# An attention and MLP kernel: one slot's score groups, two mask operands, one turn, one placing and the output buffers rearranged

## The chip, the cores and the metric

The kernel runs on one core of a Trainium2 chip. The metric is the device time of one execution in microseconds; lower is better. The engines of the core are TensorE (PE in the profile, its weight loads PEld), VectorE (DVE), ScalarE (ACT), GpSimd (POOL) and SyncE (SP). Each runs its own instructions in the order in which the program gives them, and waits on semaphores for the others. GpSimd and SyncE also issue the DMAs here.

## The reference

Attention with a forgetting decay over 8 batches, 8 heads, 576 positions and a head size of 64, and behind it an MLP whose activation is h - tanh(h):

```python
scores = scale * np.matmul(q, k.transpose(0, 1, 3, 2))
log_f = np.log(np.clip(f, 0.0001, 1.0))
cum = np.cumsum(log_f, axis=-1)
decay = cum[:, :, :, None] - cum[:, :, None, :]
scores = np.where(causal, -1000000000.0, scores + decay)
scores = scores - np.max(scores, axis=-1, keepdims=True)
attn = np.exp(scores)
attn = attn / (np.sum(attn, axis=-1, keepdims=True) + 1e-09)
x = (attn @ v), heads side by side, as 4608 rows of 512
h = x @ w_in                      # 512 x 2048
out = (h - np.tanh(h)) @ w_out    # 2048 x 512
```

## The kernel before

**Slots.** The 64 heads are worked on in 32 pairs, four to a batch. The program is a sequence of slots, one for each pair p (0 to 31) and one more to finish. In slot p the scores of pair p are made, their exponentials taken, and the values of pair p - 1 multiplied; MLP steps fill the rest. The order of all five engines is the order in which the program emits instructions (a manual schedule).

**Scores.** A pair's scores are laid into seven tiles (`TILES`, 0 to 6) of up to 512 columns, transposed: keys on the partitions, queries along the columns. Each tile has a PSUM bank, an exponential on ScalarE (L358) and, from slot 5 on, a causal mask by GpSimd on the result (L369). In slots 0 to 4 the mask is a further matmul instead (L350), of two 128 x 128 operands: `neg16`, which is -32768 on the diagonal and 0 elsewhere, and `tri16`, which is 32768 where the column is smaller than the row and 0 elsewhere. Both lie in space that weight sums use later, and are filled once at the start (L163 and L164, then L171 and L173 on GpSimd). The decay rides along as three further rows of the operands KT and QT, which come from the running sum `cum` (L178). In the slots of batch 0 tiles go in groups, `GROUPS`: g0 is tiles 0 and 1, g1 is 2 and 4, g2 is 5 and 6, g3 is tile 3. A group of two takes a double bank of a pool of two; g3 takes one of two turning banks (`t_bank`), which transposes also use.

**The hand-written order.** `FIRST` lists what slots 0 to 4 emit: `g0` to `g3` and `s0` to `s6` are score groups and tiles, `va` and `vb` the values of the two heads of the pair before, `q1` and `k1` the transposes of the next pair's q and k, `y` and `x` the turn of a finished pair's result into XR, `r` and `c` rows of constants, `m` an MLP step. From slot 5 on, `att_items` emits the seven score tiles of the slot, behind each tile the loads that `LOADS` holds for it, behind tile 1 the values and the turn of the pair before, and behind two tiles given by `TURNED` (0 and 3 where it has no entry) the transposes of q and of k for the next pair. Between these items MLP steps are spread evenly, `TAKEN` of them or 7 to 8.

**Values.** `values` makes 15 matmuls for each head (L379) into one PSUM tile; behind the second head VectorE takes the reciprocal of the sum (L385, L386) and writes `xn` (L387).

**Loads and turns.** q, k, v and the weights come in converting DMAs on GpSimd's queue. For batches 0 to 2 q and k are turned by TensorE (`trans`, L289) and copied to QT and KT by VectorE or ScalarE (L299, L297). From batch 3 on (`FAR`) they come in blocks, five for q and five for k, SyncE's queue turns them by DMA (L100) into TQ and TK, and VectorE copies them to the rows of QT and KT, four copies for each (`place`, L103: argument a is the head of a pair, c the first of two pairs). For a batch b these copies are due in the last slot of the batch before; for batch 3 that is slot 11: q behind tiles 0 and 1, k behind tiles 4 and 5, for c = 0 and c = 2 alike.

**MLP.** Finished rows are taken in nine units of 512. For each of a unit's 16 feature tiles `mlp1` makes four matmuls (L414) into a bank of a pool of three, ScalarE makes the tanh (L421), and VectorE adds it (L427) to make `gt`. The second matrix product is made of seven products of half-size blocks (`product`, L462), with sums of gt (`sums`, L441) and of the weights (`wsum`, L271). `settle` takes a product out of PSUM: three of them go to a part in SBUF, four complete a quarter of the unit's output in a tile `ost` and store it from SyncE's queue (L493). `ost` comes from the pool `tmp`, which has two buffers for each tag:

```python
ost = tmp.tile([P, DM], FP32, tag="th" if half == 0 and n == 4 else "ost", name="ost") if half != 1 else PART.pop((u, n, "ost"))
```

In the last unit two quarters are stored in halves (L486, L487), and the fourth takes a tanh buffer.

Of the kernel before, what the change touches and what calls it, by code (L numbers as in the profile page):

```python
# [8 lines left out]
FP32 = mybir.dt.float32  # L9
FP16 = mybir.dt.float16  # L10
AF = mybir.ActivationFunctionType
ALU = mybir.AluOpType
PE = mybir.EngineType.PE

PITCH = 640
VW = 66
SHIFT = 5.0
FAR = 3
BIG = 32768.0
# [4 lines left out]
def kernel(  # L24
# [10 lines left out]
    nc = tc.nc  # L35
    P = 128

    B, H, S, D = q.shape
    NH = B * H
    DM, DFF = moe_w_in.shape  # L40
    NT = B * S
    assert D == 64 and DM == H * D and S == 4 * P + 64 and H % 2 == 0
    NPAIR = H // 2
# [15 lines left out]
    smp = ctx.enter_context(tc.tile_pool(name="smp", bufs=NFT // 4))  # L59
    prt = ctx.enter_context(tc.tile_pool(name="prt", bufs=3))  # L60
    tmp = ctx.enter_context(tc.tile_pool(name="tmp", bufs=2))
    PSUM = bass.MemoryType.PSUM
    ps_av = ctx.enter_context(tc.tile_pool(name="ps_av", bufs=1, space=PSUM))
    ps_tr = ctx.enter_context(tc.tile_pool(name="ps_tr", bufs=1, space=PSUM))
# [37 lines left out]
    def place(dst, src, b, a, c):  # L102
        nc.vector.tensor_copy(out=dst[b % 2][0:D, 2 * c + a:2 * c + 3 + a:2, 0:S], in_=src[a * D:(a + 1) * D, c:c + 2, :])  # L103
# [39 lines left out]
    def load_aug(b, h0=0):  # L143
# [16 lines left out]
    nc.vector.memset(pick[0:1, 1:2], 1.0)  # L160
    nc.vector.memset(cqs[NH:P, :], 0.0)
    nc.vector.memset(KT[0][D:D + 3, 0, :], 0.0)
    nc.vector.memset(neg16, 0.0)  # L163
    nc.vector.memset(tri16, 0.0)  # L164
    nc.vector.tensor_scalar(out=lf, in0=lf, scalar1=0.0001, scalar2=1.0,
                            op0=ALU.max, op1=ALU.min)
    nc.vector.memset(QT[0][D:D + 3, 0, :], 0.0)
    nc.vector.memset(KT[0][0:D, :, S:PITCH], 0.0)
    load_qk(qn, q, 0, 4, 6)
    load_qk(kn, k, 0, 4, 6)  # L170
    nc.gpsimd.affine_select(out=neg16, in_=neg16, compare_op=ALU.not_equal,  # L171
                            fill=-BIG, base=0, pattern=[[-1, P]], channel_multiplier=1)
    nc.gpsimd.affine_select(out=tri16, in_=tri16, compare_op=ALU.is_ge,  # L173
                            fill=BIG, base=0, pattern=[[1, P]], channel_multiplier=-1)
    nc.scalar.activation(out=lf, in_=lf, func=AF.Ln)
    first = cst.tile([1, 1], FP32)
    nc.scalar.activation(out=first, in_=lf[0:1, 0:1], func=AF.Exp)
# [54 lines left out]
    def at_tile(p, ti, load):  # L232
        LOADS.setdefault((p + ti // 7, ti % 7), []).append(load)
# [10 lines left out]
    for b in range(2, B):  # L244
        p0 = (b - 1) * NPAIR
        late = 7 * (b == FAR)
        for n in range(NJ):
            at_tile(p0, (13, 15, 18, 22, 24)[n] if b == 2 else 7 + n + late, lambda b=b, n=n: load_v_part(b, n))
        if b > 2:
            at_tile(p0, 0, lambda b=b: load_aug(b))  # L250
        if b < FAR:
            continue
        for n in range(NJ):
            at_tile(p0, n - 7 + late, lambda b=b, n=n: load_block(qb, q, b, n))
            at_tile(p0, n + late, lambda b=b, n=n: load_block(kb, k, b, n))
            at_tile(p0, 4 + n + late, lambda b=b, n=n: turn_block(TQ, qb, b, n))
            at_tile(p0, 11 + n + late // 2, lambda b=b, n=n: turn_block(TK, kb, b, n))
        for n, (dst, src) in enumerate(((QT, TQ), (KT, TK))):
            for a in range(2):
                for c in (0, 2):  # L260
                    at_tile(p0 + 3, 2 * n + a + late // 3 * n, lambda b=b, dst=dst, src=src, a=a, c=c: place(dst, src, b, a, c))

    E, XN, AV, HP, GT, GP, M2, SUM, PART = {}, {}, {}, {}, {}, {}, {}, {}, {}

# [209 lines left out]
    def settle(u, n, ps, half=None):  # L474
        r0, e0 = u * UW + T2 * (n in (4, 7)), E2 * (n in (3, 7))
        if n in (1, 6, 5):
            part = prt.tile([P, DM], FP32, tag="part", name="part")
            PART[(u, n)] = part
            nc.scalar.activation(out=part, in_=ps, func=AF.Copy)  # L479
            return  # L480
        ost = tmp.tile([P, DM], FP32, tag="th" if half == 0 and n == 4 else "ost", name="ost") if half != 1 else PART.pop((u, n, "ost"))
        if half is not None:
            if half == 0:
                PART[(u, n, "ost")] = ost
            cols = slice(half * E2, half * E2 + E2)
            nc.vector.tensor_tensor(out=ost[:, cols], in0=ps[:, cols], in1=PART[(u, {7: 5, 4: 6}[n])][:, cols], op=ALU.add)  # L486
            nc.sync.dma_start(out=out[r0 + half * P:r0 + half * P + P, e0:e0 + E2], in_=ost[:, cols])  # L487
            return
        if n == 3:
            nc.scalar.activation(out=ost, in_=ps, func=AF.Copy)  # L490
        else:
            nc.vector.tensor_tensor(out=ost, in0=ps, in1=PART.pop((u, {2: 1, 7: 5, 4: 6}[n])), op=ALU.add)  # L492
        nc.sync.dma_start(out=out[r0:r0 + T2, e0:e0 + E2].rearrange("(g p) e -> p g e", p=P),  # L493
                          in_=ost.rearrange("p (g e) -> p g e", g=2))
# [15 lines left out]
    def step():  # L510
        for fn, *args in mlp[STEPS[0]]:
# [1 line left out]
        STEPS[0] += 1  # L513

    FIRST = [["8", "q0", "2", "k0", "3", "p", "s0", "s1", "q1", "s2", "k1", "s4", "s5", "q2", "s6", "s3"],
# [36 lines left out]
            else:  # L552
                spin(int(what))

    TURNED = {2 * NPAIR - 1: (3, 5), 2 * NPAIR + 1: (1, 4)}
    TAKEN = {NPAIR + 1: 5, NPAIR + 2: 5, 2 * NPAIR - 1: 5, 2 * NPAIR: 8, 2 * NPAIR + 1: 8}

    def att_items(p):
# [65 lines left out]
```

## Time and profile before

| | us |
|---|---|
| median of 3 runs | 346.81 (346.33 to 347.29) |
| the profiled execution | 345.82 |
| its span, first to last instruction | 344.1 |
| granted TensorE clock, mean | 1.000 |

The profile is of one execution. Its page gives the busy time of each engine and its share of the span; a timeline row gives an instruction's start and length, its engine and line, what it writes and reads, and in brackets how long the engine had been idle and what ended that. Busy times overlap between engines, so that an engine's idle time matters only where the others wait for it.

### The profile page before, as it was taken

How to read it: one execution, taken by the hardware profiler on the slowest of the kernel's cores; microseconds unless marked ns; L12 is line 12 of the kernel's file. 1: busy time of each engine (PE TensorE's matmuls, PEld its weight loads, DVE VectorE, ACT ScalarE, POOL GpSimd, SP SyncE). 2: the span in 40 equal slices, each digit the busy share in tenths (PEclk: the TensorE clock that was granted, in tenths of full speed). 3: DMA queues.
4: the chain of work that ended last, by engine and by line, in shares of the span. 5: the costliest groups of instructions: out<-in, count | busy, mean ns of one | idle time of the engine just before them, and what ended most of it. 6: DMA issues, size and time to landing. Idle time of an engine off the chain costs nothing.

```text
span 344.1 us, 8654 instructions
## 1 busy us (share of the span) xinstructions
PE 331.9 (96%) x3297; PEld 232.4 (68%) x3297; DVE 252.5 (73%) x521; ACT 219.4 (64%) x412; POOL 178.8 (52%) x325
## 2 busy tenths in 40 slices
PE   7899999989999999999999999999999999999996
PEld 2675557855578557887886568656887786486475
DVE  7576989749893789477965898488848864873872
ACT  6676878748655886578657875687558843633631
POOL 8987577954777637772767367742322220500500
PEclk9999999999999999999999999999999999999999
DMA  9999999999999969999999999992131013002003
GB/s 97 146 183 173 195 192 146 129 173 132 146 104 158 178 116 92 132 178 128 89 111 169 164 78 118 175 159 52 54 102 18 19 48 104 0 25 100 3 0 124
DMA packets 169560, 38.82 MB, mean 113 GB/s; under 512 B 155906, under 2 KB 169454, under 8 KB 169518
## 3 DMA queue, kind: packets, MB, share of 16 engines
q0 software_dynamic: 116576, 18.36, 86.2%
q1 hardware_dynamic: 52942, 19.90, 29.4%
q8 instruction: 26, 0.43, 0.5%
q14 instruction: 16, 0.13, 0.2%
HBM read 36.85 MB, written 9.44 MB: 135 GB/s over the span
## 4 chain that ended last, share of the span: by engine, by line
PE 80%; DVE 6%; DMA 4%; POOL 3%; ACT 2%; SPq 2%; issue 1%; POOLq 0%; DVEq 0%
PE mb L414 30%; PE px L462 16%; PE mb L462 15%; PE ps L342 11%; PE av L379 8%; DVE gt L427 2%; SPq L100 2%; DMA vn<-in_v_dram 2%; DMA TQ<-qn 1%; DMA kn<-in_k_dram 1%; ACT e L358 1%; DVE sm L441 1%; POOL vn L114 1%; ACT th L421 1%; PE t L289 1%
## 5 line engine op out<-in xcount | busy, mean ns | idle before, releaser
L414 PE MATMUL mb<-XR,win 128*128 128x512 f16 (+4 forms) x704 | 141.4, 340 | 2.1 <-DVE ost L492 1.1
L358 ACT ACTIVATE e<-ps 128x512 f16<-128x512 f32 (+1 forms) x183 | 109.0, 619 | 21.2 <-PE ps L342 13.3
L421 ACT ACTIVATE th<-mb 128x512 f32<-128x512 f32 x144 | 86.5, 601 | 53.0 <-PE mb L414 45.4
L427 DVE TENSOR_TENSOR gt<-mb,th 128x512 f16<-128x512 f32 x144 | 97.2, 687 | 23.4 <-ACT th L421 22.5
L369 POOL TENSOR_SCALAR_AFFINE_SELECT e<-e 128x128 f16<-128x128 f16 x162 | 60.2, 375 | 100.1 <-ACT e L358 99.2
L414 PEld LDWEIGHTS <-win 128*128 128x128 f16 x704 | 61.8, 97 | 50.4 <-issue 4.1
L342 PE MATMUL ps<-QT,KT 67*128 67x448 f16 (+4 forms) x376 | 73.7, 278 | 2.5 <-ACT th L421 0.8
L462 PEld LDWEIGHTS <-gt 128*128 128x128 f16 x576 | 53.8, 97 | 11.9 <-DVE gt L427 2.0
L342 PEld LDWEIGHTS <-KT 67*128 67x128 f16 x384 | 36.3, 98 | 24.6 <-DVE KT L299 2.9
L462 PEld LDWEIGHTS <-sm 128*128 128x128 f16 x432 | 40.4, 97 | 6.7 <-issue 0.4
L462 PE MATMUL mb<-ws,gt 128*128 128x256 f16 x288 | 36.4, 272 | 0.0
L379 PEld LDWEIGHTS <-e 128*128 128x128 f16 x896 | 32.1, 97 | 4.8 <-issue 1.3
L379 PE MATMUL av<-vn,e 128*128 128x65 f16 x896 | 33.8, 193 | 1.3 <-DMA vn<-in_v_dram 0.9
L492 DVE TENSOR_TENSOR ost<-mb,part 128x512 f32<-128x512 f32 x25 | 17.2, 686 | 22.7 <-PE mb L462 8.1
L479 ACT ACTIVATE part<-px 128x512 f32<-128x512 f32 x24 | 14.3, 597 | 29.7 <-PE px L462 29.7
L462 PE MATMUL px<-ws,sm 128*128 128x256 f16 x256 | 31.6, 272 | 0.0
L114 POOL DMA_DIRECT2D vn<-in_v_dram x32 | 28.5, 894 | 1.7 <-issue 1.2
L387 DVE TENSOR_TENSOR xn<-av,rs 128x640 f16<-128x640 f32 x32 | 26.4, 825 | 1.1
L441 POOL TENSOR_TENSOR sm<-gt 128x512 f16<-128x512 f16 x4 | 4.6, 1154 | 36.3 <-DVE gt L427 36.3
L95 POOL DMA_DIRECT2D qn<-in_q_dram x25 | 22.1, 883 | 1.5 <-issue 1.4
L462 PE MATMUL mb<-wout,gt 128*128 128x256 f16 x160 | 21.6, 273 | 0.7 <-DVE gt L427 0.7
L95 POOL DMA_DIRECT2D kn<-in_k_dram x25 | 21.4, 854 | 1.7 <-issue 1.6
(91 smaller groups left out, 302.4 us busy)
## 6 DMA issues: line engine op xcount, KB each, us to landing
out_dram<-ost SPq DMA_DIRECT2D x34, 256.0 KB
vn<-in_v_dram POOLq DMA_DIRECT2D x32, 128.0 KB, 6.1
qn<-in_q_dram POOLq DMA_DIRECT2D x20, 128.0 KB, 3.9
kn<-in_k_dram POOLq DMA_DIRECT2D x20, 128.0 KB, 4.5
win<-in_moe_w_in_dram POOLq DMA_DIRECT2D x4, 512.0 KB, 8.8
wout<-in_moe_w_out_dram POOLq DMA_DIRECT2D x2, 1024.0 KB, 16.4
qn<-in_q_dram POOLq DMA_DIRECT2D x10, 144.0 KB, 7.2
kn<-in_k_dram POOLq DMA_DIRECT2D x10, 144.0 KB, 6.8
```

The source lines that it names most:

```text
L95: nc.gpsimd.dma_start(out=dst[b % 2][0:pn, n, :].rearrange("p (h d) -> p h d", h=H), in_=src[b, :, n * P:n * P + pn, :].rearrange("h p d - ...
L114: nc.gpsimd.dma_start(out=vn[b % 2][:, n, h0:h1, 0:D], in_=v[b, h0:h1, n * P:(n + 1) * P, :].rearrange("h p d -> p h d"))
L342: nc.tensor.matmul(out=ps[:, col:col + n], lhsT=KT[b % 2][0:rows, h, j * P:(j + 1) * P], rhs=QT[b % 2][0:rows, h, i0:i0 + n], start=True, ...
L358: nc.scalar.activation(out=eb[:, :, lo:hi], in_=banks[:, 0:n2, lo:hi], func=AF.Exp, scale=qscale)
L369: nc.gpsimd.affine_select(out=view, in_=view, compare_op=ALU.is_ge, fill=0.0, base=0, pattern=pat, channel_multiplier=-1)
L379: nc.tensor.matmul(out=av[:, a, ib, :], lhsT=E.pop((b, c, a, j, ib)), rhs=vn[b % 2][:, j, 2 * c + a, 0:D + 1], start=(j == 0), stop=(j == ib))
L387: nc.vector.tensor_tensor(out=xn.rearrange("p i (a d) -> p a i d", a=2), in0=av[:, :, :, 0:D], in1=rs.to_broadcast([P, 2, NJ, D]), op=ALU. ...
L414: nc.tensor.matmul(out=hps[:, o:o + n], lhsT=win[:, ci, ft * P:(ft + 1) * P], rhs=XR[:, ci, t:t + n], start=(ci == 0), stop=(ci == NCH - 1))
L421: nc.scalar.activation(out=th, in_=hps, func=AF.Tanh, scale=-1.0)
L427: nc.vector.tensor_tensor(out=GT[(u, ft)], in0=hps, in1=th, op=ALU.add)
L462: nc.tensor.matmul(out=ps[:, g * E2:(g + 1) * E2], lhsT=left(k), rhs=right[:, k, :], start=(first and (g == 0 or last) and k == 0), stop=( ...
L492: nc.vector.tensor_tensor(out=ost, in0=ps, in1=PART.pop((u, {2: 1, 7: 5, 4: 6}[n])), op=ALU.add)
```

## The change

Six edits:

1. `tri16` and `neg16` are made by VectorE: `neg16` is the identity times -32768, and `tri16` a running sum along each row that starts at 32768 and adds `neg16`, so that it falls to 0 from the diagonal on. The two fills and the two GpSimd selects go. The fills of QT and KT that stood behind the clamp of f stand ahead of it.
2. In slot 1 the groups g3 and g2 come before `va` and `vb`.
3. In slot 5 the transposes of k come behind tile 2 instead of tile 3.
4. `ost` has a pool of its own, `osp`, with three buffers, and the last unit's fourth tile takes from it too.
5. For batch 3 the copies with c = 0 come behind tiles 2 and 3 (q) and 4 and 5 (k) of slot 11.
6. Those with c = 2 come behind tiles 0 and 1 (q) and 2 and 3 (k) of slot 12. The other batches stay as they were.

```diff
+    osp = ctx.enter_context(tc.tile_pool(name="osp", bufs=3))
...
     nc.vector.memset(KT[0][D:D + 3, 0, :], 0.0)
-    nc.vector.memset(neg16, 0.0)
-    nc.vector.memset(tri16, 0.0)
+    nc.vector.memset(QT[0][D:D + 3, 0, :], 0.0)
+    nc.vector.memset(KT[0][0:D, :, S:PITCH], 0.0)
     nc.vector.tensor_scalar(out=lf, in0=lf, scalar1=0.0001, scalar2=1.0,
                             op0=ALU.max, op1=ALU.min)
-    nc.vector.memset(QT[0][D:D + 3, 0, :], 0.0)
-    nc.vector.memset(KT[0][0:D, :, S:PITCH], 0.0)
+    nc.vector.tensor_scalar_mul(out=neg16, in0=id16, scalar1=-BIG)
+    nc.vector.tensor_tensor_scan(out=tri16, data0=ones16[:, 0:P], data1=neg16, initial=BIG,
+                                 op0=ALU.mult, op1=ALU.add)
     load_qk(qn, q, 0, 4, 6)
     load_qk(kn, k, 0, 4, 6)
-    nc.gpsimd.affine_select(out=neg16, in_=neg16, compare_op=ALU.not_equal,
-                            fill=-BIG, base=0, pattern=[[-1, P]], channel_multiplier=1)
-    nc.gpsimd.affine_select(out=tri16, in_=tri16, compare_op=ALU.is_ge,
-                            fill=BIG, base=0, pattern=[[1, P]], channel_multiplier=-1)
...
-                    at_tile(p0 + 3, 2 * n + a + late // 3 * n, lambda b=b, dst=dst, src=src, a=a, c=c: place(dst, src, b, a, c))
+                    o = 2 * n + a + (2 + 5 * (c > 0)) * (b == FAR)
+                    at_tile(p0 + 3, o, lambda b=b, dst=dst, src=src, a=a, c=c: place(dst, src, b, a, c))
...
-        ost = tmp.tile([P, DM], FP32, tag="th" if half == 0 and n == 4 else "ost", name="ost") if half != 1 else PART.pop((u, n, "ost"))
+        ost = osp.tile([P, DM], FP32, tag="ost", name="ost") if half != 1 else PART.pop((u, n, "ost"))
...
-             ["r", "g0", "k1", "g1", "va", "vb", "g3", "g2"],
+             ["r", "g0", "k1", "g1", "g3", "g2", "va", "vb"],
...
-    TURNED = {2 * NPAIR - 1: (3, 5), 2 * NPAIR + 1: (1, 4)}
+    TURNED = {NPAIR + 1: (0, 2), 2 * NPAIR - 1: (3, 5), 2 * NPAIR + 1: (1, 4)}
```

## The prediction, before the changed kernel ran

> **What bounds the kernel now.** I read the page first, then the busy time by stage, then TensorE's timeline for its waits, and last the engines around each wait.
>
> ```profile
> span 344.1 us, 8654 instructions
> PE 331.9 (96%) x3297; PEld 232.4 (68%) x3297; DVE 252.5 (73%) x521; ACT 219.4 (64%) x412; POOL 178.8 (52%) x325
> q0 software_dynamic: 116576, 18.36, 86.2%
> 70.00:80.00 10.00, 8.65 (x85) 5.30 (x84) 6.11 (x12) 5.23 (x12) 5.93 (x11) 1.00 1.59 169
> 80.00:90.00 10.00, 9.75 (x86) 5.26 (x85) 9.67 (x20) 7.57 (x16) 6.63 (x13) 1.00 1.91 143
> 110.00:120.00 10.00, 10.00 (x109) 6.03 (x107) 6.67 (x12) 7.46 (x15) 7.00 (x14) 1.00 2.33 165
> ```
>
> TensorE (PE) is busy 331.9 of 344.1 us, so at most 12.2 us can be won without taking work off it. A stage row gives start and end, the stage's length, then busy time of PE, PEld, DVE, ACT and POOL: from 110 us PE is full, and what is idle lies in the first 100. Its waits there:
>
> ```profile
> 8.17 0.39 PE L342 MATMUL ps<-QT,KT 67*128 67x512 f16 x1 [0.64 <-DVE KT L299]
> 14.84 0.43 PE L379 MATMUL av<-vn,e 128*128 128x65 f16 x9
> 16.17 0.31 PE L379 MATMUL av<-vn,e 128*128 128x65 f16 x5 [0.90 <-DMA vn<-in_v_dram]
> 43.55 0.39 PE L342 MATMUL ps<-QT,KT 67*128 67x512 f16 x1 [0.79 <-ACT th L421]
> 58.29 0.60 PE L462 MATMUL mb<-ws,sm 128*128 128x256 f16 x4 [0.22 <-DVE ws L271]
> 75.31 1.02 PE L414 MATMUL mb<-XR,win 128*128 128x512 f16 x4 [1.06 <-DVE ost L492]
> 77.09 1.02 PE L414 MATMUL mb<-XR,win 128*128 128x512 f16 x4 [0.29 <-DVE gt L427]
> 97.06 0.28 PE L462 MATMUL mb<-wout,gt 128*128 128x256 f16 x1 [0.36 <-DVE gt L427]
> 97.66 0.28 PE L462 MATMUL mb<-wout,gt 128*128 128x256 f16 x1 [0.32 <-DVE gt L427]
> 20.45 0.90 PE av L379 x30
> ```
>
> The number in brackets is the idle time before the row. It understates the loss: thirty value matmuls follow each other in 0.90 us on the chain of waits (0.03 each), so the nine at 14.84 fill 0.27 us, while their modelled end comes after 0.43. About 0.16 us belongs on top of each idle time.
>
> **Masks by VectorE.** Two mask selects leave GpSimd (POOL), where they stand ahead of the first v loads; two zero fills leave VectorE (DVE), which gets a multiply and a scan of 128 columns; two other fills move to an earlier pause of DVE.
>
> ```profile
> 3.64 0.45 DVE L165 TENSOR_SCALAR ws<-ws 64x576 f32<-64x576 f32 x1 [0.62 <-DMA ws<-in_f_dram]
> 4.12 0.68 ACT L175 ACTIVATE ws<-ws 64x576 f32<-64x576 f32 x1 [2.03 <-DVE ws L165]
> 4.84 1.35 DVE L178 TENSOR_TENSOR_SCAN ws<-ones,ws 64x576 f32<-64x576 f16 x1
> 7.17 0.45 POOL L171 TENSOR_SCALAR_AFFINE_SELECT ws<-ws 128x128 f16<-128x128 f16 x1
> 7.82 3.55 POOL L114 DMA_DIRECT2D vn<-in_v_dram  x4
> 11.34 5.27 DMA vn<-in_v_dram
> ```
>
> POOL issues v from 7.17 instead of 7.82, 0.65 sooner. The last v block lands at 11.34 + 5.27 = 16.6. The queue that carries it is busy for 86% of all engines' span, so an earlier issue is not an equally earlier landing: between 0 and 0.65 us, I take 0.3, near the middle. On DVE the two moved fills use the 0.62 us for which it stood for f (3.64) and what the removed fills free; only a rest beyond that would move the clamp. The new pair fits between the clamp, which ends when ACT's logarithm starts (4.12), and the running sum at 4.84, which waits for that logarithm (4.12 + 0.68 = 4.80). The scan by its length is 1.35 x 128/576 = 0.30 us, or 1.35 if nothing of it scales; the multiply lies between a tiny operation's 0.17 (17.32 below) and half of 1.19, a copy of 1152 columns (92.57 below); I take 0.2. The 0.5 fits into 0.7, so it costs nothing; at the upper ends it ends at 4.1 + 0.6 + 1.35 = 6.05 and delays the running sum by 1.2.
>
> A POOL issue beside DVE copies took longer than its siblings (0.89 each at 7.82):
>
> ```profile
> 92.34 1.17 POOL L95 DMA_DIRECT2D qn<-in_q_dram  x1
> 92.57 1.19 DVE L103 COPY QT<-TQ 64x1152 f16<-64x1152 f16 x2 [0.90 <-DMA TQ<-qn]
> ```
>
> The Trainium skill, SBUF — State Buffer, Who interferes with whom, says that a VectorE copy or tensor_scalar in a two-port mode and GpSimd share one port pair, and that the later one is blocked outright, descriptor writing included. The 0.28 us that this issue took longer agrees. By that rule the new multiply would hold up a q or k issue by up to its own 0.2 and the sum would be 4.4 instead of 4.5.
>
> **Slot 1's order.** The score groups g3 and g2 now come before both value halves.
>
> ```profile
> 14.16 1.94 ACT L358 ACTIVATE e<-ps 128x1024 f16<-128x1024 f32 x2 [0.20 <-PE ps L342]
> 17.32 0.17 DVE L385 TENSOR_SCALAR rs<-av 128x10 f32<-128x10 f32 x1 [1.98 <-PE av L379]
> 17.87 0.38 PE L342 MATMUL ps<-QT,KT 67*128 67x512 f16 x1
> 18.89 0.92 DVE L299 COPY QT<-t 64x576 f16<-64x576 f16 x2 [0.28 <-PE t L289]
> 20.23 0.46 DVE L398 COPY XR<-t 128x576 f16<-128x576 f16 x1 [0.43 <-PE t L397]
> ```
>
> Before, values run from 14.84 to about 17.1 (their end releases DVE's rs at 17.32); g3 and g2 fill the 0.75 to slot 2's start at 17.87. After, g3 starts at 14.84. g2 needs the score bank of g0, whose exponential, the first of two in 1.94, ends at about 15.2; so both groups end near 15.85, and the 0.90 of values at 16.75, with v's last block at 16.3 wanted at about that time. PE comes to slot 2 1.1 us sooner. What is late next is DVE: rs starts 16.95, 0.37 sooner, and its pauses of 0.28 and 0.43 close partly, since PE is further ahead. The k copies without which PE can't open the next slot come at the end of that DVE sequence, so from there PE gains what DVE gains. I take **0.9** for masks and order together; with v landing as before and no DVE pause closed it is 0.4, with all of PE's lead 1.1.
>
> **Slot 5's k a tile sooner.**
>
> ```profile
> 39.95 0.42 PE L289 MATMUL t<-id,kn 96*128 96x96 f16 x6
> 40.34 1.28 DVE L427 TENSOR_TENSOR gt<-mb,th 128x512 f16<-128x512 f32 x2
> 42.58 0.91 DVE L299 COPY KT<-t 64x576 f16<-64x576 f16 x2
> 45.94 0.69 DVE L427 TENSOR_TENSOR gt<-mb,th 128x512 f16<-128x512 f32 x1 [0.31 <-ACT th L421]
> 48.86 0.69 DVE L427 TENSOR_TENSOR gt<-mb,th 128x512 f16<-128x512 f32 x1 [0.44 <-ACT th L421]
> ```
>
> The copies end at 43.49, and PE starts slot 6 at 43.55: the row blames ACT, but the copy is what ended then. In the new order the six turns precede an MLP step, some 0.9 sooner than 39.95, and on DVE the copies stand before the second gt and two sums: they end near 41.0 + 0.9 = 41.9. PE's wait (0.79 + 0.16) goes. Behind the copies the second gt is now late by 0.9; nothing takes its bank before slot 6's first step. DVE then runs with only the pauses 0.31 and 0.44 up to the wsum that releases PE at 58.29, so no more than 0.75 can arrive there. I take **0.6**; the bounds are 0 and 1.0.
>
> **Three output buffers, and the placing of batch 3.**
>
> ```profile
> 67.52 8.14 SPq L493 DMA_DIRECT2D out_dram<-ost  x3
> 74.56 0.69 DVE L492 TENSOR_TENSOR ost<-mb,part 128x512 f32<-128x512 f32 x1 [3.15 <-DMA out_dram<-ost]
> 76.47 1.27 SPq L400 DMA_TRANSPOSE XR<-xn  x1
> 87.48 4.97 DMA TQ<-qn
> 91.38 3.88 SPq L100 DMA_TRANSPOSE TK<-kn  x3
> 99.20 0.91 DVE L103 COPY KT<-TK 64x1152 f16<-64x1152 f16 x2
> ```
>
> Unit 0's fourth output tile takes the second one's buffer, whose store was issued at 67.52; DVE stands 3.15 us for it, with rs, xn and the gt of the next unit behind, and SP's queue with the turns of xn and of batch 3. With three buffers it takes the first tile's, which the third tile already reused at two, so it runs near 71.4. The waits at 75.31 and 77.09 go: 1.06 + 0.29 + 2 x 0.16 = 1.67. DVE keeps 3.1 - 1.7 = 1.4 us of lead over PE, loses the 0.90 wait for TQ, and has two of its four q copies (half of 1.19, twice) moved into slot 12: the waits at 97.06 and 97.66, 0.36 + 0.32 + 0.32 = 1.0, go as well, and the 0.25 idle of the stage 80:90 with them. In sum 2.9; with the modelled ends of the waits in that stage **3.0**; between 1.7 (97 us stays) and 3.3. In the last unit the fourth tile, which took a tanh buffer for its halves, rotates through the three as well: it gets the first tile's, whose store is older than the one that the third waited for until now, so this costs nothing. The four moved copies, some 2.2 us, lie in slot 12, where PE has no wait; without that cover they would cost up to 2.2. What is late next is TK: SP's third issue starts near 94.0, lands 4.97 later at 99.0, and DVE places k at 99.20. SP's chain starts after xn's turn (76.47), which comes 2.9 sooner, so TK moves with PE but leaves no reserve.
>
> **Sum.** 0.9 + 0.6 + 3.0 = 4.5. The profiled execution took 345.82 us (344.1 of span, 1.7 around it): 341.3. It lies 1.0 below the median of the runs, 346.81; by the median the forecast is **342.3**. The bounds add to 2.1 and 5.4: 341.4 to 344.7.
>
> **Rivals.** (1) The loads set the front: v, and the q and k of the next batches, land when the busy queue lets them, PE runs into them, and the first two terms of the sum (1.5) are lost: 346.81 - 3.0 = 343.8. The 86% speaks for it; against it, among PE's waits shown behind 8 us only the one at 16.17 names a load. (2) TK lands no sooner than SP's chain lets it, DVE stands before slot 12 in place of the old waits at 97: third part 1.7, 346.81 - 3.2 = 343.6. For it speaks the 0.2 us margin, against it that SP is released as early as DVE. (3) The buffer is not what DVE waits for at 74.56, and only the front's 1.5 remains: 345.3. The row names the store, so this is weak. (4) Slower: scan and multiply cost their upper ends, the running sum comes 1.2 later, and the pause before the first score (8.17) grows from 0.64 to 1.84, longer than any shown inside the work. If the granted clock then fell to half for 10 us of matmuls, 5 us would be lost: 346.81 - 3.6 + 1.2 + 5 = 349.4. It decides at the length of that pause; pauses of 1.06 left the stage row at clock 1.00. The Trainium skill, TensorE: Matmul & The Clock Gate, What's actually happening, puts the fall at an idle window of about 3.4 us, so by it 1.84 would not suffice; no run here shows such a fall.
>
> **How the numbers follow.** A difference under 0.3% (1.04 us) is no change here. Chances: the forecast 57%, rival 1 18%, rival 2 13%, rival 3 5%, rival 4 5%, and 2% beyond. Faster: 57 + 18 + 13 and about half of rival 3's 5, less a little for unlucky runs: 89%. Same 5%, slower 6%. The range takes in the bounds and half a microsecond of spread between runs (346.33 to 347.29): 340.9 to 344.9, which leaves out rivals 3 and 4.
>
> **What would show it.** Masks: v's issue near 7.2 and no later running sum than 4.84. Slot 1: no wait of PE for vn over 0.3, slot 2 near 16.8. Slot 5: no wait of PE before slot 6, k's copies before the second gt. Buffers: no DVE wait for the output store near 71, and no PE waits from there to slot 12; if TK sets slot 12, a DVE wait for TK before the first L103 copy to KT. The forecast is wrong if PE's idle total falls by less than 2 us, or if PE's first score comes later than 8.2.

## The result, and the profile after

The changed kernel takes 343.78 us (median of 7 runs, 342.54 to 344.70) against 346.81 us for the kernel before in the same session (7 runs, 345.36 to 348.17). The ratio is 0.9912 with a 95% interval of 0.9883 to 0.9941, that is 2.0 to 4.1 us less. The profiled execution took 343.53 us, 2.29 less than that of before. The forecast was 342.3: the direction and the range held, and 1.5 us of the 4.5 that it promised did not come.

The page of the changed kernel, and its busy time by stage (start and end, length, then busy time of PE, PEld, DVE, ACT, POOL, the granted clock, DMA's busy share, and GB/s):

```profile
span 341.8 us, 8662 instructions
PE 330.5 (97%) x3297; PEld 232.2 (68%) x3297; DVE 254.5 (74%) x521; ACT 219.3 (64%) x412; POOL 178.6 (52%) x323
q0 software_dynamic: 116576, 18.36, 83.9%
...
50.00:60.00 10.00, 7.75 (x91) 5.80 (x90) 9.06 (x20) 7.28 (x15) 6.03 (x11) 1.00 2.51 150
70.00:80.00 10.00, 10.00 (x102) 6.44 (x101) 7.32 (x15) 6.94 (x14) 6.45 (x13) 1.00 2.07 181
80.00:90.00 10.00, 9.99 (x92) 5.39 (x90) 9.63 (x20) 8.05 (x18) 6.98 (x14) 1.00 1.93 147
90.00:100.00 10.00, 10.00 (x128) 7.97 (x125) 9.60 (x20) 6.42 (x13) 7.65 (x14) 1.00 1.75 135
```

From 70 to 100 us TensorE is now full, where before it stood 1.35 us in the stage from 70 and 0.25 in the stage from 80. In exchange the stage from 50 us has 2.25 us of idle time, where the kernel before has 0.43:

```profile
50.00:60.00 10.00, 9.57 (x107) 6.93 (x106) 9.76 (x21) 9.09 (x19) 7.21 (x13) 1.00 2.63 150
```

TensorE's timeline of the changed kernel names the waits; the number in brackets is the idle time ahead of the row and what ended it:

```profile
9.08 0.39 PE L341 MATMUL ps<-QT,KT 67*128 67x512 f16 x1 [1.27 <-DVE KT L298]
17.66 0.38 PE L341 MATMUL ps<-QT,KT 67*128 67x512 f16 x1
20.11 0.42 PE L288 MATMUL t<-id,kn 96*128 96x96 f16 x6 [0.46 <-DVE QT L298]
55.30 0.43 PE L288 MATMUL t<-id,qn 96*128 96x96 f16 x6 [1.66 <-DMA qn<-in_q_dram]
59.90 0.39 PE L341 MATMUL ps<-QT,KT 67*128 67x512 f16 x1 [0.42 <-ACT KT L296]
```

The first score comes 0.91 later than the 8.17 of before, slot 2 opens at 17.66 instead of 17.87, the wait for v's block is gone, the wait before slot 6 is gone, and a new one of 1.66 (1.83 with the 0.16 of the modelled end) stands at 55.30 for the load of batch 2's first q. How far each run's TensorE had come is best read where the values of a pair begin (30 matmuls for each pair). This table is worked out from the traces of before, after and eleven of the runs below (e5 is left out, whose start is another); "stage" is the time from pair 8's values to pair 11's, in which the output buffers matter:

```
                      first   values of pair                          stage
                      score   1      5      7      8      11          8 to 11
before                8.17   20.29  45.12  61.37  71.16  101.30       30.14
after                 9.08   20.37  44.26  62.35  72.14   99.04       26.90
e1_buffers            8.11   19.84  44.66  60.95  70.74   97.80       27.06
e2_place              8.11   20.54  45.36  61.62  71.41  101.02       29.61
e15_k_alone           8.14   20.57  44.57  62.32  72.11  102.33       30.22
e9_slot1              8.10   20.07  44.79  61.45  71.24  101.04       29.80
e8_masks              9.13   20.28  45.10  61.36  71.15  100.57       29.42
e4_k_later            9.19   20.47  45.19  61.45  71.25   98.14       26.89
e10_masks_early       8.30   20.29  44.18  63.69  73.48  100.38       26.90
e3_gpsimd_masks       8.09   20.19  44.09  62.83  72.62   99.52       26.90
e11_q_sooner          9.07   20.36  44.25  61.96  71.75   98.65       26.90
e12_q_sooner_gpsimd   8.10   20.02  43.92  60.18  69.97   98.09       28.12
e14_tk_sooner         8.11   19.94  44.36  62.92  72.71   99.61       26.90
```

Behind pair 11 all of them keep their distance to the end. So the change went like this: 0 at pair 1, 0.86 won at pair 5, 1.84 lost again by pair 7, and 3.24 won between pairs 8 and 11. That is 2.26 in all, and accounts for the two profiled executions (2.29). The medians differ by more, 3.03, because the profiled execution of the kernel before lies 1.0 below its median and that of the changed kernel 0.25; the table doesn't explain that part. The kernel before, e1, e2 and e15 have the same program up to slot 5, and their pair 1 begins between 19.84 and 20.57: a difference of half a microsecond there, between single profiles, says nothing.

VectorE's head of the changed kernel shows where the first score's 0.91 came from (start, length, then the operation), and GpSimd's row where v is issued:

```profile
3.60 0.45 DVE L166 TENSOR_SCALAR ws<-ws 64x576 f32<-64x576 f32 x1 [0.17 <-DMA ws<-in_f_dram]
4.80 1.35 DVE L176 TENSOR_TENSOR_SCAN ws<-ones,ws 64x576 f32<-64x576 f16 x1 [0.75 <-ACT ws L173]
...
6.68 0.75 DVE L179 SCALAR_TENSOR_TENSOR cc<-ws,cc 64x576 f16<-64x576 f32 x1
7.46 0.59 DVE L168 TENSOR_SCALAR ws<-id 128x128 f16<-128x128 f16 x1
8.09 0.42 DVE L169 TENSOR_TENSOR_SCAN ws<-ones,ws 128x128 f16<-128x128 f16 x1
8.43 1.25 DVE L298 COPY KT<-t 64x288 f16<-64x288 f16 x4
```
```profile
7.12 3.54 POOL L115 DMA_DIRECT2D vn<-in_v_dram  x4
```

The multiply (0.59) and the scan (0.42) do not stand between clamp and running sum, where VectorE idles for 0.75, but behind the last of the running sum's products, straight ahead of the four copies of k for which TensorE waits.

### The profile page after: what moved, and what is told of

It reads as the page before. It is cut to its first block, busy times and chain, and to the rows that moved or that the text cites. A ratio compares the mean times of both kernels' runs of the same rounds, so it can differ in the third digit from the quotient of the medians.

```text
span 341.8 us, 8662 instructions
## 1 busy us (share of the span) xinstructions
PE 330.5 (97%) x3297; PEld 232.2 (68%) x3297; DVE 254.5 (74%) x521; ACT 219.3 (64%) x412; POOL 178.6 (52%) x323
## 4 chain that ended last, share of the span: by engine, by line
PE 86%; DMA 6%; DVE 4%; ACT 2%; issue 1%; POOL 0%; ACTq 0%; POOLq 0%
PE mb L413 32%; PE px L461 16%; PE mb L461 15%; PE ps L341 12%; PE av L378 8%; DMA qn<-in_q_dram 5%; PE t L288 1%; ACT e L357 1%; DMA ws<-in_f_dram 1%; DVE gt L426 1%; ACT th L420 1%; DVE sm L440 1%; PE ps L349 0%; DVE xn L386 0%; DVE KT L298 0%
## 5 line engine op out<-in xcount | busy, mean ns | idle before, releaser
L491 DVE TENSOR_TENSOR ost<-mb,part 128x512 f32<-128x512 f32 x25 | 17.1, 685 | 20.6 <-PE mb L461 14.4
```

## The experiments

All ratios are to the kernel before, measured beside the run in the same session. The theory that the runs tested: the masks cost about a microsecond at the first score and slot 1's order wins it back; the third buffer alone brings the stage's 3 us; k a tile sooner pays 0.9 and loses more, because q is then late. The rivals stand in each expectation.

**e1_buffers: the kernel before with the third buffer alone.**

```
+    osp = ctx.enter_context(tc.tile_pool(name="osp", bufs=3))
...
-        ost = tmp.tile([P, DM], FP32, tag="th" if half == 0 and n == 4 else "ost", name="ost") if half != 1 else PART.pop((u, n, "ost"))
+        ost = osp.tile([P, DM], FP32, tag="ost", name="ost") if half != 1 else PART.pop((u, n, "ost"))
```

> The kernel before with the three output buffers alone (edit 4). Theory: the buffers free VectorE near 72 us, TensorE's waits of 1.06 and 0.29 us behind 75 us go, and those at 97 us as well, since VectorE then has a lead; slot 12 is reached 2.5 to 3.2 us sooner, 343.6 to 344.3 us. Rival: the lead is lost again to the head-of-line wait for TQ or TK before slot 12, which the moved placing was needed for; then 1.7 us, 345.1 us.

Measured: 343.41 us, ratio 0.9928 (0.9900 to 0.9956). Its stages and its fourth output tile:

```profile
71.02 0.69 DVE L493 TENSOR_TENSOR ost<-mb,part 128x512 f32<-128x512 f32 x1
```
```profile
70.00:80.00 10.00, 10.00 (x105) 6.07 (x103) 8.73 (x17) 6.69 (x14) 6.74 (x13) 1.00 1.75 186
80.00:90.00 10.00, 9.99 (x102) 5.60 (x99) 9.63 (x20) 7.51 (x16) 7.58 (x15) 1.00 1.68 140
90.00:100.00 10.00, 10.00 (x108) 7.94 (x107) 9.78 (x23) 5.82 (x11) 7.44 (x13) 1.00 1.81 113
```

The output tile runs at 71.02 with no idle time ahead of it, and all waits of the stage are gone, those at 97 us too, though batch 3's copies stand where they stood. The stage shrinks by 3.08 (30.14 to 27.06). The four profiles that have two buffers and nothing edited in this stage (before, e8, e9, e15) take 29.42 to 30.22 for it, so the gain is 2.4 to 3.2 us. One edit carries it, and its ratio can't be told from that of the whole change (0.9912).

**e2_place: the kernel before with the placing alone.**

```
-                    at_tile(p0 + 3, 2 * n + a + late // 3 * n, lambda ...
+                    o = 2 * n + a + (2 + 5 * (c > 0)) * (b == FAR)
+                    at_tile(p0 + 3, o, lambda ...
```

> The kernel before with only the copies of batch 3's q and k placed at other tiles, and two output buffers as ever. Theory: the waits at 75 and 77 stay (1.4 by their rows), since the fourth output tile still waits for its store; the waits at 97 go, as VectorE has two copies fewer ahead of them, which is 1.0: 345.8. Rival: without the third buffer the placing moves nothing, because the waits at 97 are the store's too: 346.8.

Measured: 345.22 us, ratio 0.9964 (0.9939 to 0.9988). TensorE's waits in the stage:

```profile
75.72 1.02 PE L415 MATMUL mb<-XR,win 128*128 128x512 f16 x4 [1.24 <-DVE ost L493]
77.50 1.02 PE L415 MATMUL mb<-XR,win 128*128 128x512 f16 x4 [0.28 <-DVE gt L428]
...
99.70 0.61 PE L343 MATMUL ps<-QT,KT 67*128 67x512 f16 x3 [0.18 <-DVE KT L103]
```

As the theory had it, the store's waits at 75 and 77 stay and those at 97 go; each of the four profiles with neither placing nor third buffer has at least one of 0.31 or more there. The stage takes 29.61, within the 29.42 to 30.22 of those four, so the profile doesn't give the size of the gain. The placing is a second cure for the same waits at 97; on top of the buffers it is worth 0.16 (27.06 to 26.90), too little to show in the times.

**e8_masks: the kernel before with the masks on VectorE alone.** The diff is the change's first edit.

> The kernel before with its masks built by VectorE and nothing else. Theory: first score at 9.1 instead of 8.17, and with values still ahead of slot 1's last score groups the loss stays: values of pair 1 start at 21.1 instead of 20.29, and the time is 0.6 to 0.9 above the kernel before. Rival: the pauses of VectorE ahead of slot 2 take the delay up, values of pair 1 start at 20.3 as before, and the time is that of the kernel before within 0.3.

Measured: 345.37 us, ratio 0.9967 (0.9946 to 0.9987). TensorE's first score:

```profile
9.13 0.39 PE L339 MATMUL ps<-QT,KT 67*128 67x512 f16 x1 [1.90 <-DVE KT L296]
```

The theory fell, the rival held: the first score is 0.96 late, and yet the values of pair 1 begin at 20.28 as before. The late start eats a wait that came anyway. In the kernel before slot 1's values begin at 14.84 and stand 0.90 for v's block at 16.17; here they begin at 16.21 and do not wait, and in both they end near 17.1. Part of that is v itself, which GpSimd issues at 7.17 here instead of 7.82. The 0.3% by which it is faster is not the front's: in the profile it lies in the stage from 8 to 11 (0.72), where nothing was edited and where runs with two buffers scatter from 29.42 to 30.22. What sets that scatter is left open.

**e9_slot1: the kernel before with slot 1's order alone.**

```
-             ["r", "g0", "k1", "g1", "va", "vb", "g3", "g2"],
+             ["r", "g0", "k1", "g1", "g3", "g2", "va", "vb"],
```

> The kernel before, with slot 1's last two score groups ahead of its values and nothing else. Theory: TensorE reaches slot 2 up to 0.7 sooner but waits there for VectorE's copies; values of pair 1 start 0 to 0.2 sooner than 20.29: 346.7, no measurable gain. Rival: the 0.9 that this order won in the changed kernel stands alone: values of pair 1 at 19.4, time 345.9.

Measured: 345.88 us, ratio 0.9983 (0.9954 to 1.0012): the median lies by the rival's 345.9, but against a kernel before of 346.66 in that session, and its interval holds no change. The trace decides for the theory: pair 1 begins at 20.07 and not at 19.4.

**e10_masks_early: the changed kernel with VectorE held to program order in the head.** The head's lines from the first fill to the running sum are put under the hand-written order that the rest of the kernel has, for VectorE alone, so that the multiply and the scan come right behind the clamp.

> The changed kernel with VectorE kept in program order over the head, so that the multiply and the scan of the masks stand before the running sum and not behind it and clo. Theory: the changed kernel's first score came at 9.08 because these two (0.59 + 0.42 us) stood ahead of k's first copies; here they delay the running sum by about 0.3, the first score comes near 8.5, slot 4 is reached 0.5 sooner than in the changed kernel, and the wait for batch 2's first q near 55 us grows by as much: 343.8 us, as the changed kernel. Rival: that wait is not a bound, the 0.5 us carries through: 343.3 us. Second rival: the masks are not what delays the first score, which stays at 9.1.

Measured: 344.51 us, ratio 0.9958 (0.9931 to 0.9984). VectorE's head, and TensorE's first score and slot 2:

```profile
4.07 0.55 DVE L169 TENSOR_SCALAR ws<-id 128x128 f16<-128x128 f16 x1
4.65 0.42 DVE L170 TENSOR_TENSOR_SCAN ws<-ones,ws 128x128 f16<-128x128 f16 x1
5.00 1.32 DVE L177 TENSOR_TENSOR_SCAN ws<-ones,ws 64x576 f32<-64x576 f16 x1
```
```profile
8.30 0.39 PE L342 MATMUL ps<-QT,KT 67*128 67x512 f16 x1 [0.66 <-DVE KT L299]
20.04 0.41 PE L289 MATMUL t<-id,kn 96*128 96x96 f16 x6 [0.47 <-DVE QT L299]
```

In the place that the prediction gave them, the two operations delay the running sum by 0.2 (4.80 to 5.00) and the first score by about as much. But 0.78 won at the first score against the changed kernel is 0.08 at pair 1. The chain of waits up to there (start, length, what) shows where it went:

```profile
9.92 6.80 DMA vn<-in_v_dram
16.77 0.31 PE av L379 x5
17.11 0.66 PE av L379 x16
...
19.43 0.47 DVE QT L299
20.04 0.29 PE t L289 x3
```

Slot 1's values start 0.58 sooner than in the changed kernel (16.18 for 16.76), wait inside for a v block that lands at 16.72, and reach their second half only 0.07 sooner (17.14 for 17.21). Behind them come VectorE's work on their result and its copies of the next q, for which slot 2's turns of k wait at 20.04, as they do at 20.11 in the changed kernel. So with the masks early v's load is the limit again, as it was in the kernel before; in the changed kernel its last block is in before TensorE wants it.

The run as a whole is not faster than the changed kernel. In six of its twelve executions, the profiled one among them, the mean granted clock was 0.990 to 0.995, and these took 344.7 to 346.0 us; the other six, at 0.998 to 1.000, took 343.0 to 344.3. The last section shows what happened in the profiled one.

**e3_gpsimd_masks: the changed kernel with the masks left on GpSimd.**

> The changed kernel with the masks built by GpSimd (its first edit undone alone). Theory: first score 8.2, values of pair 1 at 20.3 (no gain kept), q of batch 2 issued as late as in the changed kernel and landed at 55, its wait still 1.8: 343.7, same as the changed kernel within 0.3. Rival: the front ends 0.9 sooner, 342.9 if the loads follow.

Measured: 343.65 us, ratio 0.9923 (0.9894 to 0.9951), first score 8.09, pair 1 at 20.19, and the wait for batch 2's q as long as ever (pair 7 at 62.83). The theory's number. With e8, e9 and e10 the front is settled as far as single profiles can: pair 1 begins at 19.84 to 20.57 with neither edit, 20.28 with the masks, 19.94 to 20.19 with the order alone (e3, e9, e12, e14), 20.36 to 20.47 with both (after, e4, e11).

**e4_k_later: the changed kernel with slot 5's k turned where it was.**

```
-    TURNED = {NPAIR + 1: (0, 2), 2 * NPAIR - 1: (3, 5), 2 * NPAIR + 1: (1, 4)}
+    TURNED = {2 * NPAIR - 1: (3, 5), 2 * NPAIR + 1: (1, 4)}
```

> The changed kernel with k's turn in slot 5 back behind tile 3 (edit 3 undone). Theory: TensorE waits 0.8 us before slot 6 again, and waits 0.9 us less for batch 2's first q near 55 us, because that load lands when the queue lets it; no change against the changed kernel, 343.8 us. Rival: the load moves with TensorE, the turn's 0.86 us is lost: 344.6 us.

Measured: 342.64 us, ratio 0.9921 (0.9894 to 0.9947), not to be told from the 0.9912 with the edit. In the profile the wait before slot 6 is back (pair 5 at 45.19), no wait stands at 55, and pair 7 begins 0.90 sooner than in the changed kernel.

**e15_k_alone: the kernel before with that edit alone** (the same line the other way).

> The kernel before with slot 5's k turned a tile sooner and nothing else. Theory: the wait of 0.96 before slot 6 goes, and w_out's second half and batch 2's first q land 1.2 to 2 us later, at 52.8 and 55.3, so that TensorE waits 1.8 for that q: values of pair 5 start 0.86 sooner, values of pair 7 about 0.9 later than before. Rival: the late landing is chance and not this edit's (it was absent in the run with q sooner and the masks on GpSimd): q lands by 54.4, the wait at 55 is under 1.0, and values of pair 7 start no later than 61.4.

Measured: 347.10 us, ratio 1.0012 (0.9992 to 1.0033). TensorE's wait, and one microsecond of the busy time by stage in this run, in the changed kernel, in the kernel before and in e1 (the last two numbers of a row are DMA's share and GB/s):

```profile
55.27 0.43 PE L289 MATMUL t<-id,qn 96*128 96x96 f16 x6 [1.32 <-DMA qn<-in_q_dram]
```
```profile
48.00:49.00 1.00, 1.00 (x6) 0.44 (x5) 0.98 (x3) 0.77 (x2) 0.51 (x3) 1.00 1.67 108
```
```profile
48.00:49.00 1.00, 1.00 (x9) 0.55 (x7) 1.00 (x2) 0.75 (x2) 0.51 (x3) 1.00 1.74 75
```
```profile
48.00:49.00 1.00, 1.00 (x11) 0.61 (x10) 0.56 (x2) 1.00 (x4) 0.65 (x2) 1.00 1.27 210
```
```profile
48.00:49.00 1.00, 1.00 (x6) 0.48 (x5) 0.60 (x1) 0.86 (x2) 0.51 (x3) 1.00 1.19 195
```

The theory held: pair 5 starts 0.55 sooner (0.83 counted from pair 1, which came 0.28 late here), pair 7 starts 0.95 later, and nothing is won in the time. w_out's second half and then q come through the one software queue, and from 39 to 49 us the DMA engines move about 200 GB/s in the kernel before. In the changed kernel and in e15 the flow drops to 75 and 108 GB/s for the microsecond from 48. The same fall stands in e10 and e3 (69 and 62 GB/s), and in none of the six profiles without the edit (195 to 213). The engines' busy share in that microsecond does not say why: it is above that of the kernel before in three of the four and below it in e3 (0.91). About then SP issues the two turns of pair 5's xn:

```profile
47.85 1.72 SPq L400 DMA_TRANSPOSE XR<-xn  x1
```
```profile
47.41 1.22 SPq L399 DMA_TRANSPOSE XR<-xn  x1
48.68 1.23 SPq L401 DMA_TRANSPOSE XR<-xn  x1
```

The first row is the kernel before, the other two the changed kernel: where the issue was held (1.72) the load went on, where it was not (1.22) it broke off. The thirteen traces of the table above, with the landing of w_out's second half and of batch 2's first q worked out as issue plus time under way:

```
                      k a tile  length of SP's    w_out's 2nd  batch 2's
                      sooner    issue near 47.5   half lands   q lands
before                no        1.72              51.66        53.23
e1_buffers            no        2.03              51.41        53.85
e2_place              no        1.94              51.91        52.39
e9_slot1              no        1.89              51.98        54.35
e8_masks              no        1.79              52.02        53.27
e4_k_later            no        1.81              51.51        52.34
after                 yes       1.22              52.82        55.26
e10_masks_early       yes       1.22              52.74        55.26
e3_gpsimd_masks       yes       1.21              52.92        55.73
e15_k_alone           yes       1.21              53.04        55.22
e11_q_sooner          yes       1.21              56.77        49.84
e14_tk_sooner         yes       1.21              57.73        49.32
e12_q_sooner_gpsimd   yes       2.03              53.99        48.14
```

**e5_q_first: the changed kernel with batch 2's first q and k loaded ahead of w_out's second half, from the head.** The load was put ahead of the turns of batch 0's first pair, which read the same buffer, so this run computes that pair from batch 2's q and k.

```
-    for i in range(2):
-        load_wout(i * NFT // 2, (i + 1) * NFT // 2)
+    load_wout(0, NFT // 2)
+    load_qk(qn, q, 2, 0, 2)
+    load_qk(kn, k, 2, 0, 2)
+    load_wout(NFT // 2, NFT)
```

> The changed kernel with the loads of batch 2's first q and k issued ahead of the second half of w_out instead of in slot 5. Theory: TensorE's wait of 1.7 us for that q near 55 us goes, since about 1 MB less stands ahead of it; 1.0 to 1.9 us less than the changed kernel, 341.9 to 342.8 us; next late would be the second half of w_out, which VectorE needs near 55 us. Rival: the late landing was chance in one execution, and nothing changes: 343.8 us.

Measured: 381.97 us, ratio 1.1050 (1.1012 to 1.1088). A miss that answers nothing: TensorE's first turns wait for this load.

```profile
47.14 0.66 PE L290 MATMUL t<-id,qn 96*128 96x96 f16 x6 [42.17 <-DMA qn<-in_q_dram]
```

**e11_q_sooner: the same idea, with the three loads issued from slot 1, behind those turns.**

```
             elif kind == "r":
                 later_rows()
+                load_qk(qn, q, 2, 0, 2)
+                load_qk(kn, k, 2, 0, 2)
+                load_wout(NFT // 2, NFT)
```

> The changed kernel, with q and k of batch 2's first pair issued on GpSimd ahead of w_out's second half instead of after its masks in slot 5. Theory: in the changed kernel TensorE stands 1.83 us before slot 6 ends its turns at 55.3 because that q, issued behind both halves of w_out at 37.8, lands at 55.3; w_out's second half (nearly 6 us of the queue) then lands a little later without being waited for. Then the wait at 55.3 is gone, values of pair 7 start about 1.8 sooner (60.5 instead of 62.35), and the time is 342.0. Rival: the place in the queue is not what is late, the slower queue from 47 us on is; w_out's second half or the q of the second pair (57.4) then takes its place as a wait of like length, and the time stays at 343.8.

Measured: 343.26 us, ratio 0.9915 (0.9886 to 0.9944). The wait changed its name, not its length:

```profile
56.81 1.05 PE L460 MATMUL mb<-wout,gt 128*128 128x256 f16 x8 [1.61 <-DMA wout<-in_moe_w_out_dram]
```

The rival held. q now lands at 49.84, and w_out's second half, which comes behind it, at 56.77, just when the MLP wants it. Whichever of the two goes last is late, at 55.26 in the changed kernel and at 56.77 here: in these two profiles it is the queue's flow and not the order in it that stops TensorE. Here the flow is low sooner, from 43 us on (92 GB/s in the microsecond from 46), ahead of SP's issue at 47.41.

**e12_q_sooner_gpsimd: e11 with the masks left on GpSimd.**

> As the run before, but with the two masks built by GpSimd as in the kernel before (the change's first edit undone). Theory: the masks on VectorE cost 0.9 at the first score (9.08 against 8.17), and slot 1's order wins 0.9 only because it fills a wait for values that the later start makes; without the masks on VectorE the first score is at 8.2, but values of pair 1 start at 20.3 as ever, since VectorE's copies of slot 1's k end where they did: the time is within 0.2 of the run before. Rival: both sizes stand and add, values of pair 1 start at 19.4, and the time is 0.9 below the run before.

Measured: 342.79 us, ratio 0.9908 (0.9871 to 0.9945). In its profile SP's issue was held (2.03), both loads are in by 53.99, TensorE has no wait for a load behind 17 us and reaches pair 8 at 69.97, 1.19 ahead of the kernel before. Then VectorE stands for batch 3's k, and TensorE with it, by their timelines:

```profile
96.27 0.45 DVE L104 COPY KT<-TK 64x1152 f16<-64x1152 f16 x1 [1.48 <-DMA TK<-kn]
```
```profile
96.78 0.61 PE L343 MATMUL ps<-QT,KT 67*128 67x512 f16 x3 [1.06 <-DVE KT L104]
```

The two expectations can't be told apart by the time: the medians of e11 and e12 are 0.47 apart, well inside their intervals. In the profiles, that this run is 1.8 ahead of e11 at pair 7 is not the masks' doing (0.34 at pair 1, as the theory had it nearly): it goes with w_out's landing, 53.99 for 56.77.

**e14_tk_sooner: e12 with the turns of batch 3's k one tile sooner on SP's queue.**

```
-            at_tile(p0, 11 + n + late // 2, lambda ... turn_block(TK, kb, b, n))
+            at_tile(p0, 11 + n + late // 3, lambda ... turn_block(TK, kb, b, n))
```

> The run with q sooner and the masks on GpSimd, with the turns of batch 3's k issued one tile sooner on SP's queue, so that the third of five stands ahead of a slot's turn of xn. Theory: in that run VectorE stood 1.48 us for TK and TensorE 1.23 before slot 12, because TK lands at 96.2; one turn sooner lands it 1.25 sooner, the wait goes, and the time is about 1.1 below that run (341.6, ratio to the kernel before 0.9875). Rival: TK's landing is set by the loads on the other queue, the wait stays, or the turn of xn that comes 1.25 later stops the MLP instead: no gain over that run.

Measured: 342.61 us, ratio 0.9894 (0.9855 to 0.9933); not to be told from e12. Its profile cannot answer the question, since TensorE was stopped before it came that far:

```profile
57.77 1.05 PE L463 MATMUL mb<-wout,gt 128*128 128x256 f16 x8 [2.47 <-DMA wout<-in_moe_w_out_dram]
```

It answers another one. Up to 57 us e12 and e14 are the same program, 0.08 us apart at pair 1 and 0.44 at pair 5; in one w_out landed at 53.99, in the other at 57.73. So the program alone does not fix when this load lands. But neither of the two has the changed kernel's fall at 48 us (197 and 175 GB/s there). In e14 w_out's second half was issued 0.89 later (36.04 for 35.15), and the flow was low from 45 to 48 us already (135 to 155 GB/s, for 155 to 203 in e12).

With the loads in their first order, then, the fall at 48 us stands in all four profiles with slot 5's edit and in none of the six without. The three runs with moved loads don't say whether the edit forces it. What in the queues decides is open; it wasn't tried to move the turns of xn themselves.

No version tried is measurably faster than the changed kernel: the best ratios, 0.9894 and 0.9908, have intervals that hold its 0.9912.

## Why the prediction came out as it did, point by point

**Masks and slot 1's order: 0.9 forecast, 0 measured** (-0.08 at pair 1, below its lower bound of 0.4). Two steps failed. The first is "The new pair fits between the clamp ... and the running sum at 4.84 ... so it costs nothing". Their durations were mis-sized (0.59 and 0.42 for 0.2 and 0.30), but the place weighs more: the order on VectorE in the head is the compiler's, not that of the program's lines, which sets the order only from the hand-written part on (the text ahead of the prediction says it of all). The sign that the prediction asked for, a running sum no later than 4.84, came true at 4.80, and the first score was 0.91 late all the same, because the delay had moved behind the running sum. The second is "from there PE gains what DVE gains. I take 0.9". Slot 2 opened 0.21 sooner (17.66) and not the 1.1 of "PE comes to slot 2 1.1 us sooner", and of that nothing reached pair 1. e8 and e10 show, as far as single profiles can, that between the first score and pair 1 nearly nothing is passed on, in either direction: 0.96 later there is 0 later at pair 1, 0.78 sooner is 0.08 sooner. In the kernel before and in e10 slot 1's values wait for v's last blocks, and in every run VectorE's work on them and its copies of slot 2's q follow, for which TensorE waits 0.46 at 20.11 in the changed kernel. The prediction named that sequence as what is late next and then counted on its pauses to close; with 0.4 it allowed too much even at the lower end. v's issue came at 7.12 as forecast (7.17), and the multiply did not hold GpSimd's issues up, for which the prediction allowed 0.1: those of v beside it take 0.88 to 0.91 each, as before.

**Slot 5's k: 0.6 forecast, 0.9 lost in the profiles.** (The medians show no difference either way: e4's and e15's ratios above.) Its first half is exact: the copies come before the second gt, the wait of 0.79 + 0.16 before slot 6 is gone, pair 5 starts 0.86 sooner. "No more than 0.75 can arrive there. I take 0.6" then looked for the limit on VectorE up to 58.29 and not at the load that TensorE wants three microseconds earlier. That load was nowhere among the waits of before: q landed at 53.23 and was wanted at 54.33, a margin of 1.1, from which the edit itself takes 0.86 and the slower queue 2.0 more. The margin is itself uncertain: in the six profiles without the edit q lands between 52.34 and 54.35, and in e9 it already stops TensorE for 0.22. e4 and e15 show the sum of it from both sides: 0.90 and 0.95 at pair 7.

**Buffers and placing: 3.0 forecast, 3.24 measured** (2.5 to 3.3 with the scatter of the stage before). The mechanism and the size were right, the split was not: "the waits at 97.06 and 97.66 ... go as well" was put down to VectorE's lost copies and its lost wait for TQ, and e1 shows them gone with no copy moved. Since the third buffer's gain is almost the whole result, this term is why the direction was safe.

**The rivals.** Rival 1 (the loads set the front, 343.8, a chance of 18%) is what happened for the second term. For the first term it is half right: in the changed kernel VectorE's masks held the first score and no wait for v is left, but in e10, without that delay, v's load takes the lead away. That its time is the measured one to 0.02 is luck in part: it has the front unchanged, while the profiles have 0.98 lost there by pair 8 and 2.29 won in all. The 86% that spoke for it is not the share of time in which the queue was busy, as the prediction read it: it adds up packets that overlap, and between 5 and 20 us of the kernel before the same figure is 218.9%. Still the loads set more of the front than the missing waits told: a wait that does not yet show says nothing of its margin. Rival 2 (TK late before slot 12) is real but shows only in e12, whose front is at pair 8 2.2 ahead of the changed kernel's, and costs 1.22 of the stage there (28.12 against 26.90). Rival 3 is excluded by e1. Rival 4's delay of the first score came about in another way (1.27 idle ahead of it for the 1.84 feared), and the clock stayed at 1.00 there, as it did behind the 1.90 of e8.

**The signs.** Both signs by which the prediction would call itself wrong came true: the first score came later than 8.2, and TensorE's idle total, span less busy time, fell from 12.2 to 11.3 and not by 2. The first is right about the masks. The second was badly chosen: the span fell by 2.3, but the busy total of the same 3297 matmuls fell by 1.4 as well, so the difference of the two does not measure what was won. Starts of the same instructions, as in the table above, are the safer measure. Nor does all of the 12.2 lie in the first 100 us, as the prediction has it: by its stages 8.1 do, and 3.2 lie behind 340 us, in the kernel's end.

## What to carry to other kernels

A transfer that lands a microsecond before it is wanted is no wait in the profile and still the next limit: before a stage is made earlier, put the landing of every load beside the time at which it is wanted. A gain at one point is only worth what is left of it at the next point where another engine's chain ends; look for that point first, and count up to it. And test the edits of a bundle one at a time: here one of five (the placing taken as one) carried the result, one was a second cure of the same wait, and one paid itself back.

## What was not expected of the hardware

**Behind a pause of 1.9 us the clock fell to half.** In e10 TensorE waited for batch 2's q as in the changed kernel (1.74 and the 0.16 of the modelled end), and behind it the granted clock (the third number from the end) fell:

```profile
55.31 0.43 PE L289 MATMUL t<-id,qn 96*128 96x96 f16 x6 [1.74 <-DMA qn<-in_q_dram]
```
```profile
54.00:55.00 1.00, 0.00 (x0) 0.00 (x0) 0.93 (x3) 0.00 (x0) 0.79 (x2) 1.00 2.62 147
55.00:56.00 1.00, 0.69 (x9) 0.62 (x10) 1.00 (x3) 0.23 (x1) 0.45 (x1) 0.87 3.79 136
56.00:57.00 1.00, 1.00 (x7) 0.71 (x5) 1.00 (x3) 0.99 (x2) 0.24 (x1) 0.50 3.42 137
57.00:58.00 1.00, 1.00 (x6) 0.44 (x5) 1.00 (x4) 0.72 (x3) 0.00 (x0) 0.50 3.44 142
58.00:59.00 1.00, 1.00 (x7) 0.72 (x6) 1.00 (x3) 0.93 (x2) 0.50 (x1) 0.50 2.10 154
59.00:60.00 1.00, 1.00 (x14) 0.88 (x12) 0.18 (x1) 0.12 (x1) 1.00 (x3) 0.92 1.82 145
```

At half clock for 0.13/0.5 = 0.26 us of the first such row, the three full ones, and 0.08/0.5 = 0.16 of the last: 3.42 us. It cost about 1.3 (pair 6 to 7 takes 13.21 for 11.80 in the changed kernel, of which 0.08 is the longer wait), and it is why this profile is the slowest of those with the third buffer, e5 aside. Longer pauses passed without it: behind the 2.31 of e3 and the 2.47 of e14 the clock stayed at 1.00, the latter here:

```profile
57.00:58.00 1.00, 0.23 (x2) 0.21 (x3) 0.25 (x1) 0.00 (x0) 0.29 (x1) 1.00 4.18 123
58.00:59.00 1.00, 1.00 (x15) 0.93 (x13) 1.00 (x3) 0.00 (x0) 0.72 (x1) 1.00 3.81 134
```

The Trainium skill, TensorE: Matmul & The Clock Gate, What's actually happening, has a free-running window of 3413 ns: the 3.42 agrees. The same section has the clock fall after at least one idle window of about 3.4 us. That is not what this run shows, where a pause of 1.9 came before the fall, and the prediction's remark that 1.84 would not suffice is not safe. Why one pause is followed by a fall and another not is open, and executions of the kernel before, whose profile has no such pause, also came with mean clocks of 0.989 to 0.995.

**A load's flow can break off for a microsecond.** At 48 us, while SP issued turns on another queue, it fell from about 200 GB/s to between 62 and 108 in four profiles, and on the mean w_out landed 1.1 us later and q 2.1 later than in the six others with the same order of loads, which show no fall. That the turns cause it was not shown.
